# Attention into a gated MLP on one core: the hidden product of batches 1 to 7 with 512 tokens in one PSUM bank and the last 64 tokens of a batch together

## The chip, the cores and the metric

The kernel runs on one core of one Trainium2 chip. The time is device microseconds of one execution. Engines: PE multiplies matrices, and PEld, its weight loads, overlap it; DVE works on vectors, ACT evaluates functions (exponential, logarithm, sine) and copies, POOL and SP mostly issue transfers. PE writes into PSUM, which in this kernel is used as eight banks of 512 float32 values per partition; ACT and DVE read the results from there. Each engine runs its instructions in the order in which the program gives them, and waits for the others by semaphores that the framework sets.

## What is computed

```python
def _attn_ref(q, k, v, p):                     # 8 batches, 8 heads, 576 tokens, 64 per head; p has 32 rows
    p_packed = sm_attn(p, k, v)                # softmax(scale * p k^T) v
    return sm_attn(q, p_packed, p_packed)      # softmax(scale * q p_packed^T) p_packed

def _moe_ref(x, w_in, w_out):                  # x is 4608 x 512, w_in 512 x 2048, w_out 2048 x 512
    h = x @ w_in
    g = h * np.cos(h)
    return g @ w_out
```

The output of the attention, its heads side by side, is `x`: 8 batches of 576 tokens.

## The kernel before

**Batches and steps.** All loops are unrolled, and the program's order is written out by hand. The first attention of a batch gives `p_packed`; the kernel multiplies it with `w_in` at once (`ppw`, L201), so that the hidden product of a batch is h = PPW times a2n, where a2n holds the normalised weights of the second attention (256 rows, as two halves `y` of 128) for 576 tokens. PPW is made in four parts n of 512 of the 2048 hidden columns. h is made in 16 steps `fc` of 128 hidden columns. A step is two accumulating products (y = 0, 1), then a cosine on ACT (a sine with a shift of pi/2), then a multiplication h * cos(h) on DVE into `gT`. The output product (`out_gen`, L343, matmuls on L351) takes 128 tokens at a time, as 16 matmuls of 512 columns.

**Two forms of a step.** `h_mm` (L256) takes all 576 tokens, as two halves of 288 tokens (a bank takes no more than 512), in a pair of banks: four matmuls, one cosine and one multiplication of 576 columns. It serves batches 1 to 7. `h_one` (L283) takes the first 512 tokens in one bank: two matmuls. The last 64 tokens of all 16 steps are then done together by `h_rest` (L298): 32 matmuls of 64 columns into one pair, one cosine of 1024 columns and one multiplication of 1024. These two serve batch 0.

**The joint tile.** 576 is four times 128 and 64 over. The last 64 tokens of an even batch and the next odd one are put side by side into `joint`, which is a fifth group of 128 tokens for the odd batch. `h_mm` has POOL copy them from `gT` into `joint` after steps 7 and 15 (L274); `h_rest` multiplies straight into it (L309).

**Banks.** Two banks (`O`) serve the output product. The other six are grouped by `banks(pairs)` (L54): it closes the pools of the old grouping and opens `pairs` pairs (`psA`, handed out in turn) and single banks (`psH`, `one()`) from the rest. Batch 0's steps run with `banks(0)`, six singles; from L472 on, `banks(3)`, three pairs, holds to the end. `bank()` takes one of the two `O` banks for other uses.

**A batch's period, from batch 2 on.** Ahead of the slot: the scores of the second attention (`s2`, matmuls on L143, into two pairs; in the period of batch 2 they come a little later, and the scores of the first attention, `s1`, stand at the front), the first two parts of PPW, the next batch's scores, the sums (`sums2`), `normalise` into a2n, and between them portions of the previous batch's output product, `fill(n)`, n matmuls each. Then `slot` (L487): sixteen h steps, with the rest of the output product spread between them by a quota; `heavy` gives a step a larger quota, a part of which comes behind the step's extra work (the hooks). `keep` output matmuls are left for the time after the slot. The hook `tiled` at step 7 makes the third and fourth part of PPW (L213) and the next batch's packed values (`pp`, L186), the latter in the unused end of the pair of step 7 (`spare`). `last`, which stands between the matmuls and the multiplication of step 15, transposes these values (`pp_T`, L198). In slot 1 the hooks are others: `pw2` at step 2, `h_rest(0)` at 4, `pack_p` at 6, transposes of k at 8 and 10.

**Order on the engines around a slot's end.** PE: the matmuls of step 15, the two of `pp_T`, the output matmuls left by the quota, those of `fill(5)` (`fill(4)` before `s1(2)`), the scores, a part of PPW. DVE: the multiplication of step 14, the copy of `ppT`, the multiplication of step 15. ACT: the cosine of step 15, a table load, the exponentials of the scores. POOL: the copies into `joint`, then a copy of one element (`behind`, L96) that waits for a transposing transfer, then loads.

Of the kernel before, what the change touches and what calls it, by code (L numbers as in the profile page):

```python
# [15 lines left out]
def kernel(  # L16
# [37 lines left out]
    def banks(pairs):  # L54

        psum["stack"].close()
        if pairs:
            psum["A"] = psum["stack"].enter_context(tc.tile_pool(name="psA", bufs=pairs, space=PSUM))
        if pairs < 3:
            psum["H"] = psum["stack"].enter_context(tc.tile_pool(name="psH", bufs=6 - 2 * pairs, space=PSUM))  # L60
# [28 lines left out]
    def psa(dt=FP32):  # L89
        return psum["A"].tile([128, 2, 512 if dt == FP32 else 1024], dt, name="psA", tag="A")  # L90
# [32 lines left out]
    def bank(dt=FP32):  # L123
        return O.tile([128, 512 if dt == FP32 else 1024], dt, name="ot", tag="ot")
# [54 lines left out]
    def pp(b, eng=V, own=None):  # L179

        ps = own() if own else psa()[:, 0, :]
        for y in range(2):
            for j in range(C):
                c = 2 * (j % 3) + j // 3
                for x in range(4):
                    nc.tensor.matmul(ps[32 * x:32 * x + 32, y * D:(y + 1) * D],  # L186
                                     a1T[b][0:TP, y, j, 32 * x:32 * x + 32],
                                     bf["v", b][:, 2 * x + y, c * D:(c + 1) * D],
                                     start=(j == 0), stop=(j == C - 1))
        t = pp_sb[b % 2].rearrange("p a d -> p (a d)")  # L190
        copy(eng, t[:, 0:2 * D], ps[:, 0:2 * D])
        copy(eng, t[:, 2 * D:3 * D], ps[:, 0:D])
# [5 lines left out]
            nc.tensor.transpose(ps[:, i * 128:(i + 1) * 128], t[:, i * D:i * D + 128], ident)  # L198
        copy(eng, ppT[b % 2].rearrange("p i x n -> p (i x n)"), ps[:, 0:256])

    def ppw(b, n, eng=None, own=False, later=False, cuts=((0, 512),)):  # L201
        if b not in PPW:
            PPW[b] = ppw_pool.tile([128, 2, DF], BF16, name="PPW", tag="PPW")
        two = isinstance(eng, tuple)
        if own:
            ps = [bank(), bank()]
        else:
            t = psa()
            ps = [t[:, 0, :], t[:, 1, :]]
        for x in range(4):  # L210
            for y in range(2):
                r = slice(64 * y, 64 * y + 64)
                nc.tensor.matmul(ps[y][32 * x:32 * x + 32, :], ppT[b % 2][r, 0, x, :],  # L213
                                 w_in_bf[r, x, n * 512:(n + 1) * 512], start=True, stop=True)

        def evacuate(cuts=cuts):
            if own or two:
                for a, z in cuts:
                    for y in range(2):
                        copy(eng[y] if two else eng, PPW[b][:, y, n * 512 + a:n * 512 + z], ps[y][:, a:z])  # L220
            else:
                copy(eng or (V, ACT)[n % 2], PPW[b][:, :, n * 512:(n + 1) * 512], t)
        if later:
            return [lambda c=c: evacuate((c,)) for c in cuts]
        evacuate()
# [25 lines left out]

    gT, joint = {}, {}

    spare = [None]

    def h_mm(b, fc):  # L256
        if fc == 0:
            g_tile(b)
        ps = psa()
        spare[0] = ps[:, 1, HS:512]  # L260
        for y in range(2):
            for e in range(2):
                nc.tensor.matmul(ps[:, e, 0:HS], PPW[b][:, y, fc * 128:(fc + 1) * 128],  # L263
                                 a2n[b][:, y, e * HS:(e + 1) * HS], start=(y == 0), stop=(y == 1))
        cs = cos_pool.tile([128, S], BF16, name="cosT")
        csv = cs.rearrange("p (e x) -> p e x", e=2)
        ACT.activation(out=csv, in_=ps[:, :, 0:HS], func=AF.Sin, bias=PI_HALF)  # L267

        def rest():
            V.tensor_tensor(out=gT[b][:, fc, :].rearrange("p (e x) -> p e x", e=2),  # L270
                            in0=ps[:, :, 0:HS], in1=csv, op=ALU.mult)
            if fc % 8 == 7:
                j0 = (b % 2) * 64
                G.tensor_copy(out=joint[b // 2][:, fc - 7:fc + 1, j0:j0 + 64],  # L274
                              in_=gT[b][:, fc - 7:fc + 1, 512:576])
        return rest

    def g_tile(b):
        gT[b] = g_pool.tile([128, NFC, S], BF16, name="gT", tag="gT")
        if b % 2 == 0:  # L280
            joint[b // 2] = j_pool.tile([128, NFC, 128], BF16, name="joint", tag="joint")

# [15 lines left out]
    def h_rest(b):  # L298

        t = psa()  # L300
        for fc in range(NFC):
            for y in range(2):
                nc.tensor.matmul(t[:, fc // 8, (fc % 8) * 64:(fc % 8) * 64 + 64],  # L303
                                 PPW[b][:, y, fc * 128:(fc + 1) * 128], a2n[b][:, y, 512:576],
                                 start=(y == 0), stop=(y == 1))
        cs = cos_pool.tile([128, 2, 512], BF16, name="cosR", bufs=1)
        ACT.activation(out=cs, in_=t, func=AF.Sin, bias=PI_HALF)
        j0 = (b % 2) * 64
        V.tensor_tensor(out=joint[b // 2][:, :, j0:j0 + 64],  # L309
                        in0=t.rearrange("p a (f x) -> p (a f) x", x=64),  # L310
                        in1=cs.rearrange("p a (f x) -> p (a f) x", x=64), op=ALU.mult)
# [53 lines left out]
    def to_do():  # L365
        return sum(n for _, n in filler)
# [73 lines left out]
    normalise(0)  # L440
    s1(1)
    ACT.preload_act_table_set(SIN_SET)
    cut_ppw, rest_ppw = ppw(0, 0, V, own=True, later=True, cuts=((0, 128), (128, 512)))
    warm(3, psa()[:, 0, :])
    cut_ppw()
    rest_ppw()
# [3 lines left out]
    for fc in range(13):  # L450
        h_one(0, fc)()()
        if fc in (0, 4, 8):
            ppw(0, 1 + fc // 4, (ACT, ACT if fc == 8 else V), own=True)
    c13 = h_one(0, 13)
    pp(1, ACT, own=bank)
    c13()()
# [30 lines left out]
    def slot(s, hooks, keep=0, heavy={}, last=None):  # L487


        left = to_do() - keep  # L490
        weight = [1 + heavy.get(fc, (0, 0))[0] for fc in range(NFC)]
        for fc in range(NFC):
            rest = h_mm(s, fc)
            if fc == NFC - 1 and last:
                last()
            rest()
            quota = (left * sum(weight[:fc + 1])) // sum(weight) - (left + keep - to_do())
            behind = min(quota, heavy[fc][1]) if fc in heavy else quota
            fill(quota - behind)
            while hooks and hooks[0][0] == fc:  # L500
                hooks.pop(0)[1]()
            fill(behind)

    def pw2(b, n, eng=None):
        ppw(b, n, eng)
        ppw(b, n + 1, eng)

    def tiled(b):


        own, later = spare[0], []
        for n in (2, 3):
            later += ppw(b, n, (ACT, V)[n - 2], later=True)
        later[0]()
        pp(b + 1, V, own=lambda: own)
        later[1]()

    def tk2():
# [8 lines left out]
    def cross(n, b):  # L527
        return lambda: xbar(n, b)

    osb_eng[0] = ACT  # L530
    slot(1, [(2, lambda: pw2(1, 2, (ACT, V))), (4, lambda: h_rest(0)), (6, lambda: pack_p(2, 4)), (7, cross("k", 3)),
             (8, tk2), (9, cross("q", 2)), (10, lambda: pe_T("k", 2, (V, V, ACT), (2,)))], 4, {2: (1, 2), 4: (3, 5)})
    ACT.preload_act_table_set(EXP_SET)
    osb_eng[0] = V
    behind(xT["q", 2][0:1, 0, 0:1])
    load("v", 3)
# [35 lines left out]
        load(n, b)  # L572
    fill(9)
    osb_eng[0] = ACT
    slot(2, [(7, lambda: tiled(2))], 10, {7: (5, 4)}, lambda: pp_T(3, V))

    for s in range(3, B):
        nxt = s + 1 < B
        ACT.preload_act_table_set(EXP_SET)
        osb_eng[0] = V  # L580
        set_filler(s - 1)
        fill(5)
        s2(s)
        ppw(s, 0, V)
        fill(8 if nxt else 9)
        if nxt:
            s1(s + 1)
            ppw(s, 1, V)
            a1_xbar(s + 1)
            xbar("q", s + 1)  # L590
            recips(s + 1)
            if s + 2 < B:
                xbar("k", s + 2)
                behind(xT["k", s + 2][0:1, 0, 0:1])
        else:
            for n in range(1, 4):
                ppw(s, n, V)
        fill(4 if nxt else 5)
        sums2(s, 0)
        fill(5)  # L600
        sums2(s, 1)
        normalise(s)
        ACT.preload_act_table_set(SIN_SET)
        fill(13)
        osb_eng[0] = ACT
        for n, b in (("v", s + 2), ("q", s + 2), ("k", s + 3)):
            if b < B:
                load(n, b)
        if nxt:
            slot(s, [(7, lambda: tiled(s))], 5 if s % 2 else 13, {7: (5, 4)}, lambda: pp_T(s + 1, V))  # L610
        else:
            slot(s, [], 5)
    set_filler(B - 1)
    fill(1000)
    tail_chunk(B - 1, 4)
# [30 lines left out]
```

## Time and profile before

| | |
|---|---|
| median of 3 runs | 244.99 us (244.93 to 245.46) |
| the profiled execution | 245.1 us, of which 243.3 us from the first to the last instruction |
| granted TensorE clock | 0.997 |
| output matmuls, L351, on `gT` | 512, 134.0 us busy |
| cosines, L267 | 112, 72.9 us busy, 652 ns each |
| multiplications, L270 | 112, 83.3 us busy, 757 ns each |
| copies into `joint`, L274 | 14, 8.6 us busy, 618 ns each |
| cosine of `h_rest(0)`, L307 | 1, 1023 ns |
| multiplication of `h_rest(0)`, L309 | 1, 1225 ns |

Slot 1 runs from about 40 to 60 us of the span, slot 2 from 74 to 90, slot 3 from 100 to 116, slots 4 to 6 at 126, 152 and 179, slot 7 from 206 to 221; then comes the output product of batch 7. Busy time of a group is the time in which any of its instructions ran; a mean is from the start to the end of one, so that means add up to more than the busy time where instructions overlap, as they do on PE. "Idle before" is time in which the engine had nothing to do ahead of the group's instructions, with what ended it.

### The profile page before, as it was taken

To read this page: it belongs to the slowest core of one execution; us is meant where nothing else is said; L and a number is where in the kernel's file an instruction comes from. 1 tells how busy PE (TensorE), PEld (TensorE's weight loads), DVE (VectorE), ACT (ScalarE), POOL (GpSimd) and SP (SyncE) were. 2 spreads that over 40 slices of the span, in tenths; PEclk is the share of its full clock that TensorE was granted. 3 is DMA by queue.
4 is the path that set the end of the run, shared out by engine and by line. 5 is a ranking of instruction groups with operands and counts; after the bars stand their busy time and mean duration, and the time that the engine had idled before them with its cause. 6 is when DMAs were issued, how large, how long until landed. Compare 5 with 4: busy or idle time off the path is not lost.

```text
span 243.3 us, 5484 instructions
## 1 busy us (share of the span) xinstructions
PE 233.8 (96%) x2251; PEld 128.9 (53%) x2251; DVE 162.0 (67%) x256; ACT 166.1 (68%) x267; POOL 37.4 (15%) x60
## 2 busy tenths in 40 slices
PE   7789899999999999999999999999999999999994
PEld 3454354566446564556455654655455645665453
DVE  3259997787568795778758675868667878784001
ACT  2349999778478696868787687858796666773110
POOL 8432230210400041004100510030101010011000
PEclk9999999999999999999999999999999999999998
DMA  6999999999799999997999899999292111311133
GB/s 94 203 205 206 204 206 229 199 237 187 163 184 183 219 179 180 197 197 163 158 199 219 162 221 204 188 164 176 66 192 52 31 46 43 86 36 53 46 84 86
DMA packets 64377, 37.37 MB, mean 154 GB/s; under 512 B 36865, under 2 KB 59777, under 8 KB 64353
## 3 DMA queue, kind: packets, MB, share of 16 engines
q0 software_dynamic: 23152, 18.75, 51.0%
q1 hardware_dynamic: 40960, 18.16, 35.9%
q8 instruction: 17, 0.28, 0.4%
q10 hardware_dynamic: 240, 0.13, 0.2%
q14 instruction: 8, 0.06, 0.1%
HBM read 37.22 MB, written 9.44 MB: 192 GB/s over the span
## 4 chain that ended last, share of the span: by engine, by line
PE 82%; DVE 6%; ACT 1%; issue 1%; ACTq 0%
PE ot L351 50%; PE psA L263 22%; DVE gT L295 3%; PE psA L213 3%; PE psA L143 2%; PE psA L239 2%; PE ot L337 1%; PE psA L186 1%; DVE gT L270 1%; DVE PPW L87 1%; ACT cosT L267 1%; ACT cosT L294 0%; PE psA L116 0%; DVE qT L87 0%; PE psA L303 0%
## 5 line engine op out<-in xcount | busy, mean ns | idle before, releaser
L351 PE MATMUL ot<-w_out_bf,gT 128*128 128x512 bf16 x512 | 134.0, 379 | 0.0
L270 DVE TENSOR_TENSOR gT<-psA,cosT 128x576 bf16<-128x576 f32 x112 | 83.3, 757 | 21.0 <-ACT cosT L267 19.9
L267 ACT ACTIVATE cosT<-psA 128x576 bf16<-128x576 f32 x112 | 72.9, 652 | 24.9 <-PE psA L263 23.5
L263 PE MATMUL psA<-a2n,PPW 128*128 128x288 bf16 x448 | 73.3, 286 | 0.0
L351 PEld LDWEIGHTS <-gT 128*128 128x128 bf16 x512 | 48.2, 98 | 39.5 <-issue 4.2
L263 PEld LDWEIGHTS <-PPW 128*128 128x128 bf16 x448 | 43.8, 98 | 30.1 <-issue 0.4
L87 DVE CAST PPW<-psA 128x1024 bf16<-128x1024 f32 (+1 forms) x24 | 26.8, 1131 | 6.4 <-PE psA L213 6.2
L85 ACT COPY osb<-ot 128x512 f32<-128x512 f32 (+1 forms) x23 | 13.1, 569 | 16.2 <-PE ot L351 13.9
L87 DVE COPY osb<-ot 128x512 f32<-128x512 f32 (+2 forms) x15 | 9.7, 645 | 20.4 <-PE ot L337 17.2
L274 POOL COPY joint<-gT 128x512 bf16<-128x512 bf16 x14 | 8.6, 618 | 78.2 <-DVE gT L270 78.2
L249 DVE SCALAR_TENSOR_TENSOR a2n<-a2u,r,lns 128x576 bf16<-128x576 bf16 x16 | 12.4, 814 | 9.6 <-ACT lns L247 9.6
L152 ACT ACTIVATE a<-psA 128x576 bf16<-128x576 f32 x16 | 10.2, 646 | 8.2 <-PE psA L143 8.2
L241 ACT ACTIVATE lns<-psA 128x576 f32<-128x576 f32 x16 | 10.3, 650 | 7.2 <-PE psA L239 6.7
L351 PE MATMUL ot<-w_out_bf,joint 128*128 128x512 bf16 x48 | 12.2, 380 | 0.0
L98 POOL COPY gate<-kT 1x1 bf16<-1x1 bf16 x4 | 0.7, 180 | 72.7 <-DMA kT<-kbf 72.7
L231 ACT ACTIVATE a2u<-psA,rs 128x576 bf16<-128x576 f32 x16 | 11.0, 737 | 1.1 <-PE psA L143 1.0
L247 ACT ACTIVATE lns<-lns 128x576 f32<-128x576 f32 x16 | 10.0, 673 | 0.0
L213 PE MATMUL psA<-w_in_bf,ppT 64*32 64x512 bf16 x224 | 9.8, 379 | 0.0
L295 DVE TENSOR_TENSOR gT<-psH,cosT 128x512 bf16<-128x512 f32 x15 | 9.3, 680 | 0.4 <-ACT cosT L294 0.4
L391 PE MATMUL ot<-wz 128*128 128x512 f32 (+2 forms) x13 | 7.5, 661 | 1.9 <-DVE wz L404 1.7
L294 ACT ACTIVATE cosT<-psH 128x512 bf16<-128x512 f32 x15 | 8.4, 628 | 0.7 <-DVE gT L295 0.4
L289 PE MATMUL psH<-a2n,PPW 128*128 128x512 bf16 x30 | 7.8, 381 | 0.8 <-DVE PPW L87 0.8
(88 smaller groups left out, 170.6 us busy)
## 6 DMA issues: line engine op xcount, KB each, us to landing
kbf<-in_k_dram POOLq DMA_DIRECT2D x8, 576.0 KB, 14.0
vbf<-in_v_dram POOLq DMA_DIRECT2D x8, 576.0 KB, 7.8
qbf<-in_q_dram POOLq DMA_DIRECT2D x8, 576.0 KB, 10.9
out_dram<-osb SPq DMA_DIRECT2D x24, 192.0 KB, 2.6
out_dram<-osb SPq DMA_DIRECT2D x22, 128.0 KB, 2.9
w_in_bf<-in_moe_w_in_dram POOLq DMA_DIRECT2D x4, 512.0 KB, 17.3
w_out_bf<-in_moe_w_out_dram POOLq DMA_DIRECT2D x4, 512.0 KB, 20.8
out_dram<-osb SPq DMA_DIRECT2D x25, 64.0 KB, 2.3
```

Of the source, the lines that this page charges most:

```text
L85: ACT.copy(out=out, in_=in_)
L87: eng.tensor_copy(out=out, in_=in_)
L152: ACT.activation(out=a1[b % 2][:, y, :, 0:TP].rearrange("p (e m) x -> p e m x", e=2), in_=ps[y][:, :, 0:HS].rearrange("p e (m x) -> p e m ...
L213: nc.tensor.matmul(ps[y][32 * x:32 * x + 32, :], ppT[b % 2][r, 0, x, :], w_in_bf[r, x, n * 512:(n + 1) * 512], start=True, stop=True)
L231: ACT.activation(out=a2u[b][:, y].rearrange("p (e x) -> p e x", e=2), in_=ps[y][:, :, 0:HS], func=AF.Exp, scale=rs1[b][:, y:y + 1])
L241: ACT.activation(out=lns[b][:, y].rearrange("p (e x) -> p e x", e=2), in_=ps[:, :, 0:HS], func=AF.Ln)
L249: V.scalar_tensor_tensor(out=a2n[b][:, y], in0=a2u[b][:, y], scalar=r1[b][:, y:y + 1], in1=lns[b][:, y], op0=ALU.mult, op1=ALU.mult)
L263: nc.tensor.matmul(ps[:, e, 0:HS], PPW[b][:, y, fc * 128:(fc + 1) * 128], a2n[b][:, y, e * HS:(e + 1) * HS], start=(y == 0), stop=(y == 1))
L267: ACT.activation(out=csv, in_=ps[:, :, 0:HS], func=AF.Sin, bias=PI_HALF)
L270: V.tensor_tensor(out=gT[b][:, fc, :].rearrange("p (e x) -> p e x", e=2), in0=ps[:, :, 0:HS], in1=csv, op=ALU.mult)
L295: return lambda: V.tensor_tensor(out=gT[b][:, fc, 0:512], in0=ps, in1=cs, op=ALU.mult)
L351: nc.tensor.matmul(pss[c], w, w_out_bf[:, fc, :], start=(fc == 0), stop=(fc == NFC - 1))
```

## The change

Batches 1 to 7 take the form that batch 0 had. `h_mm` and `spare` go; a slot begins with `banks(1)`, one pair and four singles, its steps are `h_one(s, fc)`, each in one single, and `h_rest(s)` comes as a hook: behind step 13 in slot 1, behind step 11 in slots 2 to 7. Ahead of the next batch's scores `banks(3)` makes three pairs again. `gT` shrinks to 512 tokens, and POOL's copies into `joint` go. Within a slot, the fourth part of PPW takes two singles instead of a pair (`own=one`), so it leaves them by two copies of 512 columns rather than one of 1024; the third part has the pair, `pp` and `pp_T` take a single each; `pack_p` and one of the transposes of k in slot 1 do so too. In slot 2 the quota at step 7 becomes (6, 3): a larger share of the output matmuls goes there, three of them behind the hook.

```diff
@@ ppw @@
-    def ppw(b, n, eng=None, own=False, later=False, cuts=((0, 512),)):
+    def ppw(b, n, eng=None, own=None, later=False, cuts=((0, 512),)):
...
         if own:
-            ps = [bank(), bank()]
+            ps = [own(), own()]
@@ h @@
-    spare = [None]
-
-    def h_mm(b, fc):
-        if fc == 0:
-            g_tile(b)
-        ps = psa()
-        spare[0] = ps[:, 1, HS:512]
-        for y in range(2):
-            for e in range(2):
-                nc.tensor.matmul(ps[:, e, 0:HS], PPW[b][:, y, fc * 128:(fc + 1) * 128],
-                                 a2n[b][:, y, e * HS:(e + 1) * HS], start=(y == 0), stop=(y == 1))
-        cs = cos_pool.tile([128, S], BF16, name="cosT")
-        csv = cs.rearrange("p (e x) -> p e x", e=2)
-        ACT.activation(out=csv, in_=ps[:, :, 0:HS], func=AF.Sin, bias=PI_HALF)
-
-        def rest():
-            V.tensor_tensor(out=gT[b][:, fc, :].rearrange("p (e x) -> p e x", e=2),
-                            in0=ps[:, :, 0:HS], in1=csv, op=ALU.mult)
-            if fc % 8 == 7:
-                j0 = (b % 2) * 64
-                G.tensor_copy(out=joint[b // 2][:, fc - 7:fc + 1, j0:j0 + 64],
-                              in_=gT[b][:, fc - 7:fc + 1, 512:576])
-        return rest
-
     def g_tile(b):
-        gT[b] = g_pool.tile([128, NFC, S], BF16, name="gT", tag="gT")
+        gT[b] = g_pool.tile([128, NFC, 512], BF16, name="gT", tag="gT")
@@ slot @@
+        banks(1)
         left = to_do() - keep
...
-            rest = h_mm(s, fc)
+            rest = h_one(s, fc)()
@@ pw2, tiled @@
         ppw(b, n, eng)
-        ppw(b, n + 1, eng)
+        ppw(b, n + 1, eng, own=one)
...
-        own, later = spare[0], []
-        for n in (2, 3):
-            later += ppw(b, n, (ACT, V)[n - 2], later=True)
+        later = ppw(b, 2, ACT, later=True) + ppw(b, 3, V, own=one, later=True)
         later[0]()
-        pp(b + 1, V, own=lambda: own)
+        pp(b + 1, V, own=one)
         later[1]()
@@ slot 1 @@
-    slot(1, [(2, lambda: pw2(1, 2, (ACT, V))), (4, lambda: h_rest(0)), (6, lambda: pack_p(2, 4)), (7, cross("k", 3)),
-             (8, tk2), (9, cross("q", 2)), (10, lambda: pe_T("k", 2, (V, V, ACT), (2,)))], 4, {2: (1, 2), 4: (3, 5)})
+    slot(1, [(2, lambda: pw2(1, 2, (ACT, V))), (4, lambda: h_rest(0)), (6, lambda: pack_p(2, 4, one(BF16))), (7, cross("k", 3)),
+             (8, tk2), (9, cross("q", 2)), (10, lambda: pe_T("k", 2, (V, V, ACT), (2,), own=one)), (13, lambda: h_rest(1))], 4, {2: (1, 2), 4: (3, 5)})
     ACT.preload_act_table_set(EXP_SET)
+    banks(3)
@@ slot 2 @@
-    slot(2, [(7, lambda: tiled(2))], 10, {7: (5, 4)}, lambda: pp_T(3, V))
+    slot(2, [(7, lambda: tiled(2)), (11, lambda: h_rest(2))], 10, {7: (6, 3)}, lambda: pp_T(3, V, own=one))
@@ batches 3 to 7 @@
         ACT.preload_act_table_set(EXP_SET)
+        banks(3)
...
-            slot(s, [(7, lambda: tiled(s))], 5 if s % 2 else 13, {7: (5, 4)}, lambda: pp_T(s + 1, V))
+            slot(s, [(7, lambda: tiled(s)), (11, lambda: h_rest(s))], 5 if s % 2 else 13, {7: (5, 4)},
+                 lambda: pp_T(s + 1, V, own=one))
         else:
-            slot(s, [], 5)
+            slot(s, [(11, lambda: h_rest(s))], 5)
```

The calls of `ppw` for batch 0 say `own=bank` in place of `own=True`, which is the same.

More of the change, by code (lines that the diff above doesn't have):

```diff
@@ L442 @@
     ACT.preload_act_table_set(SIN_SET)
-    cut_ppw, rest_ppw = ppw(0, 0, V, own=True, later=True, cuts=((0, 128), (128, 512)))
+    cut_ppw, rest_ppw = ppw(0, 0, V, own=bank, later=True, cuts=((0, 128), (128, 512)))
     warm(3, psa()[:, 0, :])
@@ L452 @@
         if fc in (0, 4, 8):
-            ppw(0, 1 + fc // 4, (ACT, ACT if fc == 8 else V), own=True)
+            ppw(0, 1 + fc // 4, (ACT, ACT if fc == 8 else V), own=bank)
     c13 = h_one(0, 13)
```

## The prediction

> **What bounds it now.** I read the page's totals, then the groups by line with shapes kept apart, then the chain that ended last in order of time, then the timeline around three places. In the groups below the columns are: line, engine, operation, output<-inputs, shapes, count, busy us and mean ns of one, idle before.
>
> ```profile
> span 243.3 us, 5484 instructions
> PE 233.8 (96%) x2251; PEld 128.9 (53%) x2251; DVE 162.0 (67%) x256; ACT 166.1 (68%) x267; POOL 37.4 (15%) x60
> ...
> L263 PE MATMUL psA<-a2n,PPW 128*128 128x288 bf16 x448 | 73.3, 286 | 0.0
> ...
> L295 DVE TENSOR_TENSOR gT<-psH,cosT 128x512 bf16<-128x512 f32 x15 | 9.3, 680 | 0.4 <-ACT cosT L294 0.4
> ```
>
> PE is busy 96% of the span and its two big groups (L351, L263) stand with no idle time before them. Means of PE mislead, since matmuls overlap; the chain gives what each costs in a full stream:
>
> ```profile
> 46.95 0.93 PE psA L303 x32
> ...
> 115.25 0.49 PE psA L263 x4
> 115.74 0.17 PE psA L198 x2
> 115.92 1.51 PE ot L351 x7
> 117.43 0.37 PE psA L143 x16
> ```
>
> (start, us, what.) A 288-column matmul of h takes 0.49/4 = 0.123 us, a 512-column one 1.51/7 = 0.216, and one of 64 columns 0.93/32 = 0.029. In the stretch from slot 2 to slot 7 nearly every piece of the chain is PE. So only two things count: PE's own work, and any wait put on PE.
>
> **PE's work does not change.** The old h step is 4 x 288 columns, 0.49 us; the new one is 2 x 512, 2 x 0.216 = 0.43. Sixteen of them save 16 x (0.49 - 0.432) = 0.93 us a batch. The added `h_rest` is 32 matmuls, which L303 prices at 0.93. The sum is 0.00 for each of the seven batches; the number of matmuls and weight loads is the same.
> The Trainium skill, "TensorE: Matmul & The Clock Gate", section "LDWEIGHTS (loading the stationary operand)", says that a weight load takes its columns divided by 1.2 GHz and so would make 32 matmuls of 64 columns cost their loads; the L303 piece (0.93 us for 32) is against that here, and it stands below as a rival.
>
> **ACT, DVE, POOL.** On DVE, back to back, an old step takes 0.71 us (two in 1.43 in the chain), a new one 9.3/15 = 0.62; 16 x 0.09 = 1.5 us saved, and one multiplication of 1.23 us (L309, seen once) added. On ACT 0.65 against 0.56 (8.4 us for 15), and one cosine of 1.02 (L307) added. Both engines are busy about three quarters of a slot (12.8 and 12.0 us of the 16.2 us of slot 3), so this lies beside PE's matmuls as a total, and uncovered it would cost at most the 1.23 us a batch; what matters is that 1.02 and 1.23 us come in one lump at step 11, four steps before the slot's end. The POOL copies (L274, 14 x 0.62 us) go; POOL waits 78 us for DVE before them, and behind them stands only the next gate copy, which waits 72.7 us for a transpose anyway. No DMA is added or moved: nothing.
>
> **The stall that goes.** In slot 2 the values for batch 3 (L186) wait for the multiplication of step 7, whose pair they share:
>
> ```profile
> 80.67 1.42 DVE L270 TENSOR_TENSOR gT<-psA,cosT 128x576 bf16<-128x576 f32 x2 [0.27 <-ACT cosT L267]
> ...
> 81.34 0.63 PE L213 MATMUL psA<-w_in_bf,ppT 64*32 64x512 bf16 x16
> ...
> 82.15 0.55 PE L186 MATMUL psA<-vbf,a1T 96*32 96x64 bf16 x48 [0.18 <-DVE gT L270]
> ```
>
> L213 takes 0.55 where nothing waits (107.37 to 107.92 in slot 3), so 0.26 us is lost. After, they use the single bank of step 6: -0.26. The other slots have no such wait.
>
> **The stall that comes.** At each slot's end the banks are regrouped from one pair and four singles to three pairs, and the scores (L143) are the first work in the new grouping. Does that first matmul wait for its own two banks only, or for everything in the old grouping? Before has one comparable regrouping, six singles to three pairs at 35 us:
>
> ```profile
> 33.80 0.86 ACT L85 COPY qT<-psH 128x768 bf16<-128x768 bf16 x1
> 34.11 1.02 DVE L87 COPY qT<-psH 128x768 bf16<-128x768 bf16 x2
> 34.25 0.81 PE L391 MATMUL psH<-wz 128*128 128x512 bf16 x3
> ...
> 35.24 0.17 PEld L143 LDWEIGHTS <-ppT 64*32 64x32 bf16 x16 [0.68 <-ACT qT L85]
> 35.27 0.44 PE L143 MATMUL psA<-qT,ppT 64*32 64x288 bf16 x16 [0.21 <-DVE qT L87]
> ```
>
> Counting 22 singles handed out in turn, the last DVE copy (ends 35.13) reads the third bank, and the first score matmuls write the first two and read only the columns that ACT's copy wrote by 34.66. PE's own work was streamed by 34.25 + 3 x 0.216 = 34.9. Yet all 16 start at 35.24, 0.11 us behind that last copy. That data alone is not the reason is seen in slot 3: step 8 starts at 109.29 on the third part of PPW while DVE writes the fourth until 110.11. So I take it that a regrouping waits for all of the old banks. Inside one grouping it waits bank by bank:
>
> ```profile
> 143.15 0.76 DVE L270 TENSOR_TENSOR gT<-psA,cosT 128x576 bf16<-128x576 f32 x1
> 143.87 0.14 PEld L143 LDWEIGHTS <-ppT 64*32 64x32 bf16 x16 [0.42 <-issue]
> ```
>
> There the scores began before step 15's multiplication had ended (143.91). After, they would wait for it, and it is later, because of the lump. From the end of step 11's matmuls in slot 3 (us): h_rest done 0.93; cosine 0.97 to 1.99; its multiplication 2.03 to 3.25; DVE then runs without a gap (0.62 each, the last 0.07 overlapping): steps 12, 13, 14 begin at 3.18, 3.80, 4.41, the ppT copy at 5.03, step 15 at 5.27 and ends at 5.95. PE meanwhile: 0.93 + 4 x 0.432 + 7 output matmuls x 0.216 = 4.17 at the end of step 15. Before, the scores start 117.36 - 115.74 = 1.62 us behind that point, so they are due at 5.79 and get leave at 5.95 + 0.14 (35.13 to 35.27) = 6.09: **0.30 us lost**. Slots 3 to 6 each have seven output matmuls in that stretch: 4 x 0.30 = 1.20. In slot 2 the new weights (6, 3) leave only five: step 15 ends at 3.74; the ppT transposes need the single of step 12, free at 3.18 + 0.68 + 0.14 = 4.00, and lose 0.35; the scores are due at 5.71: 0.38 more, 0.73 in all. In slot 1 h_rest stands at step 13: step 15 ends at 0.93 + 0.86 + 0.86 = 2.65, its multiplication at 4.48, the scores are due 1.44 behind (60.47 to 61.91): 4.62 - 4.09 = 0.52. Behind the waiting matmul stand PPW's first part and all output matmuls; nothing of it is made up, since PE has no slack later. The regrouping at a slot's beginning costs nothing: the last readers of the pairs are the logarithms, which a2n, and so step 0, needs anyway. **Bounds**: if I am wrong on bank by bank, 0; if DVE is 0.2 us later or earlier at each of the six ends, 2.45 - 1.2 = 1.25 to 2.45 + 1.2 = 3.65.
>
> Two small edits are bounded by nothing and 0.1: PPW's fourth part as two 512-column copies on DVE (2 x 0.60 against 1.22), and step 9, which now waits for the first of them: due 1.5 us behind L186's end, released at 0.15 + 0.33 + 0.60 + 0.14 = 1.2. I take 0.
>
> **Sum.** 1.20 + 0.73 + 0.52 - 0.26 = +2.19 on a span of 243.3, so 245.5; the profiled execution took 245.1 with 1.8 around its span, 0.1 above the median of 244.99. Median after: 244.99 + 2.19 = **247.2**. Its own range: 244.99 + 1.25 - 0.26 = 246.0 to 244.99 + 3.65 = 248.6.
>
> **Rivals.**
> (a) *Waits bank by bank even across the regrouping.* Then the scores' first pair is h_rest's, long free, the second holds steps 13 and 14, and only PPW's first part (0.25 us behind the scores) meets step 15: 4 x 0.05 + 0.13, plus 0.35 in slot 2, less 0.26: +0.4, so **245.4**. For it: the row at 143.87. Against: 35.24. It decides if the releaser of L143 is not step 15.
> (b) *Faster.* Four singles let step n run until the multiplication of step n-4, not n-3, has ended, and DVE has 0.3 us less a slot. Its place is the starts around L213, L186 and L143, its price the waits hidden there: from 35.27 to 239.77 all matmuls at stream rates (560 x 0.216, 448 x 0.123, the rest by their pieces) make about 202.5 us against 204.5, so 2.0 at most; half of it gives **244.0**. It decides if (a)'s releases hold and those 0.42 us gaps before weight loads are waits. Against: the gaps carry "issue", and slots 3 to 6 have no wait for DVE in them.
> (c) *The weight loads of h_rest bind*: 32 x 98 ns (PEld, L303) = 3.1 instead of 0.93, seven times 2.2: **260**. Against it is L303's own piece. That is the rule of the page named above.
>
> **Chances.** Forecast 0.60, (a) 0.24, (b) 0.14, (c) 0.01, a larger stall 0.01. A measurement here tells 0.2% (0.49 us) from nothing. Slower: 0.60 + 0.04 of (a) + 0.02 = 0.66; same: 0.18 of (a); faster: 0.14 + 0.02 of (a) = 0.16. The range takes in (a): 244.6 to 248.6.
>
> **What would show it.** PE's busy time as before (233.8) while the span grows by about 2 us; L143's weight loads released by DVE gT L295, 0.3 to 0.7 us each at five or six ends, and the chain leaving PE there through the multiplications from L309 on; no wait at L186 in slot 2; L303 at 0.93 each of seven new times. If L143 waits for nothing, the step on the regrouping is wrong; if step 15 ends sooner than 1.6 us behind its matmuls, the lump is.

## The result, and the profile after

The changed kernel takes 248.03 us (median of 4 runs, 247.95 to 248.09) against 245.01 (4 runs): a ratio of 1.0119, 95% interval 1.0102 to 1.0137. It is slower by 3.0 us where 2.2 were forecast.

The page's totals of the changed kernel:

```profile
span 246.2 us, 5480 instructions
PE 233.4 (95%) x2251; PEld 112.9 (46%) x2251; DVE 161.8 (66%) x268; ACT 166.4 (68%) x274; POOL 28.9 (12%) x46
```

PE is as busy as before (233.4 against 233.8) while the span grew by 2.9 us: the loss is idle time of PE. Two places hold it. The first was not in the forecast; it is the beginning of slot 1, in the timeline (start, us, engine, line, operation, output<-input, shapes, count, idle before and its releaser):

```profile
39.17 1.55 DVE L249 SCALAR_TENSOR_TENSOR a2n<-a2u,r,lns 128x576 bf16<-128x576 bf16 x2 [1.81 <-ACT lns L247]
...
40.63 1.28 DVE L87 CAST PPW<-psA 128x512 bf16<-128x512 f32 x2
42.03 0.13 PEld L265 LDWEIGHTS <-PPW 128*128 128x128 bf16 x2 [2.05 <-issue]
42.06 0.59 PE L265 MATMUL psH<-a2n,PPW 128*128 128x512 bf16 x2 [1.58 <-DVE PPW L87]
```

The same place in the profile of before:

```profile
39.09 1.55 DVE L249 SCALAR_TENSOR_TENSOR a2n<-a2u,r,lns 128x576 bf16<-128x576 bf16 x2 [1.81 <-ACT lns L247]
...
40.23 0.86 PE L263 MATMUL psA<-a2n,PPW 128*128 128x288 bf16 x4
...
40.55 1.28 DVE L87 CAST PPW<-psA 128x512 bf16<-128x512 f32 x2
```

L263 is the matmul of the old step, L265 that of the new one, in a single (`psH`). Step 0 can start when the first half of a2n is there; before, it did, at 40.23. Now it starts at 42.06, just behind two copies of PPW's second part, which it doesn't read; nor, if the pools lie in the order in which they are opened, does it overwrite the banks that they read.

The second is the end of a slot. This is the chain of waits around the end of slot 5 (start, us, what):

```profile
167.18 0.95 PE psA L279 x32
...
168.15 1.03 ACT cosR L283
...
169.21 1.23 DVE joint L285
170.43 1.65 DVE gT L271 x3
...
172.42 0.61 DVE gT L271
...
173.07 0.44 PE psA L143 x16
```

L279 is `h_rest`, L283 and L285 its cosine and its multiplication, L271 a step's multiplication, L143 the scores. Before, all pieces there were PE's. Now the chain leaves PE with `h_rest`, goes through ACT and DVE, and comes back at the scores, 0.04 us behind the last multiplication.

Each start of a first score matmul (from the timelines), and the distance to the one before it:

| | before | after | distance grew by |
|---|---|---|---|
| s2(1) | 35.27 | 35.36 | |
| s1(2), behind slot 1 | 61.91 | 63.81 | 1.81 |
| s2(3), behind slot 2 | 91.43 | 93.58 | 0.25 |
| s2(4), behind slot 3 | 117.36 | 119.65 | 0.14 |
| s2(5), behind slot 4 | 143.87 | 146.36 | 0.20 |
| s2(6), behind slot 5 | 170.38 | 173.07 | 0.20 |
| s2(7), behind slot 6 | 196.89 | 199.78 | 0.20 |

The sum is 2.80 us, and 0.09 lie ahead of s2(1).

Slot 2 needs a closer look, since its 0.25 is a sum of gains and losses. Its end before, and after:

```profile
89.09 0.65 PE L263 MATMUL psA<-a2n,PPW 128*128 128x288 bf16 x4
89.72 0.27 PE L198 MATMUL psA<-ident,pp_sb 128*128 128x128 bf16 x2
```

```profile
90.83 0.59 PE L265 MATMUL psH<-a2n,PPW 128*128 128x512 bf16 x2
91.59 0.27 PE L198 MATMUL psH<-ident,pp_sb 128*128 128x128 bf16 x2 [0.16 <-DVE gT L271]
91.70 1.67 PE L327 MATMUL ot<-w_out_bf,joint 128*128 128x512 bf16 x7
93.58 0.44 PE L143 MATMUL psA<-qT,ppT 64*32 64x288 bf16 x16 [0.21 <-DVE gT L271]
```

PE's means overlap, so the waits are read from start to start. After, the transposes of `ppT` (L198) start 0.76 us behind step 15, where 0.43 is usual (117.33 to 117.76 in slot 3): 0.33 lost. Before, it was 0.63 where 0.49 is usual (141.66 to 142.15 in slot 4): 0.14 were lost there already. The scores start 1.88 us behind the first of the seven output matmuls, where 1.60 is usual (89.83 to 91.43 before): 0.28 lost. L186 no longer waits its 0.26. Together 0.33 - 0.14 + 0.28 - 0.26 = 0.21, of the 0.25 in the table.

### The profile page after: what moved, and what is told of

It is laid out like the page before. It is cut to its first block, busy times and chain, and to the rows that moved or that the text cites. A ratio compares the mean times of both kernels' runs of the same rounds, so it can differ in the third digit from the quotient of the medians.

```text
span 246.2 us, 5480 instructions
## 1 busy us (share of the span) xinstructions
PE 233.4 (95%) x2251; PEld 112.9 (46%) x2251; DVE 161.8 (66%) x268; ACT 166.4 (68%) x274; POOL 28.9 (12%) x46
## 4 chain that ended last, share of the span: by engine, by line
PE 69%; DVE 14%; ACT 4%; DMA 2%; issue 1%; ACTq 0%
PE ot L327 41%; PE psH L265 16%; DVE gT L271 8%; PE psA L279 3%; DVE joint L285 2%; PE psA L213 2%; DMA out_dram<-osb 2%; PE psA L143 2%; ACT cosR L283 2%; PE ot L313 1%; DVE PPW L87 1%; PE psA L239 1%; PE psH L186 1%; DVE a2n L249 1%; ACT a2u L231 1%
## 5 line engine op out<-in xcount | busy, mean ns | idle before, releaser
L271 DVE TENSOR_TENSOR gT<-psH,cosT 128x512 bf16<-128x512 f32 x127 | 84.4, 688 | 18.3 <-ACT cosT L270 17.4
L270 ACT ACTIVATE cosT<-psH 128x512 bf16<-128x512 f32 x127 | 75.1, 603 | 23.0 <-PE psH L265 21.3
L265 PE MATMUL psH<-a2n,PPW 128*128 128x512 bf16 x254 | 74.6, 380 | 2.4 <-DVE PPW L87 2.4
L265 PEld LDWEIGHTS <-PPW 128*128 128x128 bf16 x256 | 24.5, 98 | 32.9 <-issue 2.7
L87 DVE CAST PPW<-psA 128x1024 bf16<-128x1024 f32 (+1 forms) x18 | 20.2, 1134 | 6.9 <-PE psA L213 6.4
L285 DVE TENSOR_TENSOR joint<-psA,cosR 128x1024 bf16<-128x1024 f32 x8 | 9.8, 1225 | 6.1 <-ACT cosR L283 6.1
L283 ACT ACTIVATE cosR<-psA 128x1024 bf16<-128x1024 f32 x8 | 8.2, 1023 | 3.0 <-PE psA L279 3.0
L279 PEld LDWEIGHTS <-PPW 128*128 128x128 bf16 x256 | 8.6, 98 | 1.9
L279 PE MATMUL psA<-a2n,PPW 128*128 128x64 bf16 x256 | 8.8, 193 | 0.0
L367 PE MATMUL ot<-wz 128*128 128x512 f32 (+2 forms) x13 | 6.9, 619 | 1.9 <-DVE wz L380 1.7
L213 PE MATMUL psA<-w_in_bf,ppT 64*32 64x512 bf16 x176 | 8.5, 380 | 0.0
```

What stands on the lines that cost most here:

```text
L87: eng.tensor_copy(out=out, in_=in_)
L265: nc.tensor.matmul(ps, PPW[b][:, y, fc * 128:(fc + 1) * 128], a2n[b][:, y, 0:512], start=(y == 0), stop=(y == 1))
L270: ACT.activation(out=cs, in_=ps, func=AF.Sin, bias=PI_HALF)
L271: return lambda: V.tensor_tensor(out=gT[b][:, fc, 0:512], in0=ps, in1=cs, op=ALU.mult)
L285: V.tensor_tensor(out=joint[b // 2][:, :, j0:j0 + 64], in0=t.rearrange("p a (f x) -> p (a f) x", x=64), in1=cs.rearrange("p a (f x) -> p ( ...
```

## The experiments

Two theories. **The regrouping**: closing the pools of one grouping of banks and opening those of another makes the first matmul in a new pool wait until everything that read the old banks has ended, whichever bank it itself uses. **Bank by bank**: each tile waits for its own banks, and the loss lies in the new steps or in the lump that `h_rest` puts on ACT and DVE, whatever the pools.

### The kernel before, its grouping closed and opened again

At a slot's beginning (`e1_reopen_start`):

```diff
     def slot(s, hooks, keep=0, heavy={}, last=None):
+        banks(3)
         left = to_do() - keep
```

> The kernel before, with its three pairs closed and opened again as the same three pairs at each slot's beginning; no other instruction changes. If opening a grouping waits for every reader of the old one, step 0 of slot 1 must wait for the late copies of PPW's second part on DVE, which end at 41.83 in the trace of before, instead of starting at 40.23: +1.5 us, in slot 1 alone (in the later slots those copies are over long before), so 246.5. If waits go bank by bank, nothing changes: 245.0.

Measured: 246.65 us against 245.18 (ratio 1.0059, interval 1.0042 to 1.0076): +1.47. The timeline of this run:

```profile
40.52 1.28 DVE L87 CAST PPW<-psA 128x512 bf16<-128x512 f32 x2
41.91 0.37 PEld L263 LDWEIGHTS <-PPW 128*128 128x128 bf16 x4 [1.99 <-issue]
41.94 0.65 PE L263 MATMUL psA<-a2n,PPW 128*128 128x288 bf16 x4 [1.53 <-DVE PPW L87]
```

These are the old steps in the old pairs. In slot 1 every tile also has its old pair: six pairs have been handed out since L472, so the turn stands at the first one with or without the reopening. The only thing done is to close and reopen, and step 0 waits for the copies. Bank by bank falls with this.

At the slots' ends (`e2_reopen_end`):

```diff
     ACT.preload_act_table_set(EXP_SET)
+    banks(3)
     osb_eng[0] = V
...
         ACT.preload_act_table_set(EXP_SET)
+        banks(3)
         osb_eng[0] = V
```

> The kernel before, with its three pairs closed and opened again as the same three pairs behind each of slots 1 to 6. If opening a grouping waits for every reader of the old one, the scores wait for step 15's multiplication, which in before ends 0.05 us ahead to 0.04 us behind their start, plus 0.14 us of signal: 0.18, 0.08, 0.00, 0.18, 0.07 and 0.18 us at the six ends, +0.7 in all, so 245.7. Bank by bank: 245.0. It shows what a regrouping costs where nothing lumpy stands ahead of it.

Measured: 245.32 against 245.18 (1.0013, 0.9999 to 1.0027): 0.1, not 0.7. The wait is there, but shorter than I took it. The timeline at the end of slot 4:

```profile
143.03 0.76 DVE L270 TENSOR_TENSOR gT<-psA,cosT 128x576 bf16<-128x576 f32 x1
143.84 0.14 PEld L143 LDWEIGHTS <-ppT 64*32 64x32 bf16 x16 [0.51 <-DVE gT L270]
```

The multiplication ends at 143.79 and the scores start at 143.84, 0.05 us later; I had counted 0.14. The distances of the table grow by 0.08, 0.09 and 0.10 at the ends of slots 1, 4 and 6 and by 0.01 or nothing at the others; at the end of slot 3 the scores wait for nothing (their usual 0.42 us gap). So a regrouping by itself costs a slot's end at most 0.1 us in the old kernel.

### The changed kernel with the late copies moved up

`e3_ppw_early`:

```diff
     fill(3)
+    rest_ppw()
     normalise(1)
     ACT.preload_act_table_set(SIN_SET)
-    rest_ppw()
```

> The changed kernel, with the copies of PPW's second part of batch 1 ahead of the normalisation instead of behind it. If step 0 of slot 1 waits for these copies because of the regrouping (42.06 in the trace of after, 40.23 in before), it now waits only for a2n, which comes some 0.3 us later since DVE does the copies first: 1.4 us come back, 246.6. If the start of slot 1 is late for another reason (single banks as such, the weights), it stays at 248.0.

Measured: 246.61 us (1.0061, 1.0046 to 1.0076 of before), 1.42 under the changed kernel. The start of slot 1 was 1.4 us of the 3.0; the table says the same, 1.81 less the 0.39 that the next run finds at that slot's end.

### The changed kernel with the lump two steps earlier

`e4_rest_early`:

```diff
-    ... (13, lambda: h_rest(1)) ...
+    ... (11, lambda: h_rest(1)) ...
...
-    ... (11, lambda: h_rest(2)) ...
+    ... (9, lambda: h_rest(2)) ...
...
-    ... (11, lambda: h_rest(s)) ...
+    ... (9, lambda: h_rest(s)) ...
```

The last of these stands twice, in the call for slots 3 to 6 and in that for slot 7.

> The changed kernel, with the last 64 tokens of a batch two steps earlier in each slot (step 9 instead of 11, in slot 1 step 11 instead of 13). If the waits at the slots' ends come from the lump of 1.02 us on ACT and 1.23 us on DVE that stands four steps ahead of the end, DVE has caught up by then, and the scores wait at most 0.05 to 0.1 us: about 1.2 us come back, 246.8. If the regrouping costs the same whatever stands ahead of it, it stays at 248.0.

Measured: 246.55 us (1.0057, 1.0042 to 1.0072), 1.48 under the changed kernel. The end of slot 3 in its timeline:

```profile
114.69 3.07 DVE L271 TENSOR_TENSOR gT<-psH,cosT 128x512 bf16<-128x512 f32 x5
...
117.68 0.28 DVE L87 COPY ppT<-psH 128x256 bf16<-128x256 bf16 x1
...
117.88 0.68 DVE L271 TENSOR_TENSOR gT<-psH,cosT 128x512 bf16<-128x512 f32 x1
118.76 0.14 PEld L143 LDWEIGHTS <-ppT 64*32 64x32 bf16 x16 [0.42 <-DVE gT L271]
```

Step 15's multiplication ends at 118.56, 0.2 us ahead of the scores; in the changed kernel it ended 0.06 us ahead of them and held them. The distances between the scores fall by 0.39, 0.31 and four times 0.16 or 0.17 against the changed kernel. The regrouping alone is not enough for a wait at a slot's end: it takes a DVE that is late, and in slots 1 and 3 to 6 the lump made it so.

Slot 2 is different. What came back there is the wait of the transposes (L198), not that of the scores:

```profile
90.98 1.67 PE L327 MATMUL ot<-w_out_bf,joint 128*128 128x512 bf16 x7
92.86 0.44 PE L143 MATMUL psA<-qT,ppT 64*32 64x288 bf16 x16 [0.21 <-DVE gT L271]
```

The scores start 1.88 us behind the start of the output matmuls, as in the changed kernel: 0.28 us too late. Two steps are not enough for DVE to catch up there.

### Both, and a pair that stays open

`e5_both_early` is the two edits together.

> The changed kernel with both: the copies of PPW's second part of batch 1 ahead of the normalisation, and the last 64 tokens two steps earlier in each slot. If the loss is made of two separate waits at regroupings, what each edit alone brought back adds: 1.42 + 1.48 = 2.90 of the 3.0 us, so 245.1, level with the kernel before. If both edits ease the same wait, less: 246.0 or more.

Measured: 245.36 against 245.15 (1.0003, 0.9987 to 1.0019). The edits add up; what remains is level with the kernel before.

`e6_pair_open` leaves both late things where they are and takes one pair out of the regrouping:

```diff
     def banks(pairs):
...
-        if pairs:
+        psum["k"], psum["pairs"] = 0, pairs
+        if psum.get("first") == "due":
+            psum["first"] = ctx.enter_context(tc.tile_pool(name="psF", bufs=1, space=PSUM))
+        if psum.get("first"):
+            if pairs == 3:
+                psum["A"] = psum["stack"].enter_context(tc.tile_pool(name="psA", bufs=2, space=PSUM))
+        elif pairs:
...
     def psa(dt=FP32):
+        k = psum["k"]
+        psum["k"] += 1
+        if psum.get("first") and (k % 3 == 0 or psum["pairs"] == 1):
+            return psum["first"].tile([128, 2, 512 if dt == FP32 else 1024], dt, name="psF", tag="F")
         return psum["A"].tile([128, 2, 512 if dt == FP32 else 1024], dt, name="psA", tag="A")
...
+    psum["first"] = "due"
     banks(3)
...
+    psum["stack"].close()
```

> The changed kernel, with one pair of banks in a pool of its own that is never closed, and only the other four banks regrouped (two pairs or four singles). The order of the work and the bank of each tile stay. The first four heads of the scores behind a slot go to that pair. If it is the closing and opening that makes the scores wait, they now wait for h_rest's multiplication only, and the other four heads, 0.2 us later, for step 15: the waits of 0.4, 0.5 and 4 x 0.2 us at the six ends fall by about 0.2 each, 1.2 in all: 246.8. The start of slot 1 stays late, since PPW's second part lies in the regrouped banks. If the scores wait because of the lump as such, whatever the pools, it stays at 248.0.

Measured: 247.25 us (1.0074, 1.0047 to 1.01), 0.8 under the changed kernel, of 1.2 expected. The timeline shows what the total can't (`psF` is the pair that stays open; lines stand ten further down):

```profile
118.73 0.68 DVE L281 TENSOR_TENSOR gT<-psH,cosT 128x512 bf16<-128x512 f32 x1
119.30 0.28 PEld L153 LDWEIGHTS <-ppT 64*32 64x32 bf16 x16 [0.42 <-DVE ppT L93]
119.30 0.32 PE L153 MATMUL psF<-qT,ppT 64*32 64x288 bf16 x8
...
119.47 0.32 PE L153 MATMUL psA<-qT,ppT 64*32 64x288 bf16 x8
```

The first eight matmuls of the scores, into the open pair, start while step 15's multiplication still runs (it ends at 119.41). The other eight, into a pair that was opened anew, start 0.06 us behind it. At the end of slot 1 it is plainer: the first eight start at 63.47, the others at 63.87, again 0.05 us behind the end of the multiplication, where 0.13 us lie between them when nothing waits. Same engine, same instruction, same moment: the pool decides. Their banks don't explain it: by the count of singles handed out in slot 1, step 15 has the fourth, and these eight go to the pair made of the first two (if pools lie in the order in which they are opened, which no trace shows). The total gained less than expected because the second eight still wait: only the 0.13 us of the first eight come before them, and slots 3 to 6 had only 0.17 or 0.18 to give.

`e7_all` is all three edits.

> All three edits together. What is left of the waits at the slots' ends after the first two (0.2 us in slot 2, 0.1 or less in the others) should go, and the stall that the change took out of slot 2 (0.26 us) then shows: 244.7 to 244.9, a little under the kernel before. If the single banks cost something by themselves, it stays above 245.0.

Measured: 245.23 against 245.15 (1.0004, 0.9982 to 1.0025): not under the kernel before. From s2(1) to s1(2) it takes 26.87 us where before took 26.64: the early copies make a2n late, and step 0 waits 0.3 us for it. From there to s2(4) it takes 55.23 where before took 55.45. Gone from slot 2 are L186's wait of 0.26 and the 0.14 that the transposes of `ppT` lost before; the second eight of the scores still wait 0.15 there (91.46, where 91.31 would do).

`e8_ppw_in_pair` therefore puts the copies back behind the normalisation, and PPW's second part into the pair that stays open:

```diff
+    psum["k"] = 6
     rest_ppw, = ppw(1, 1, (V, V), later=True)
     fill(3)
-    rest_ppw()
     normalise(1)
     ACT.preload_act_table_set(SIN_SET)
+    rest_ppw()
```

The lines are marked against `e7_all`; the count 6 makes the next pair handed out the open one.

> One pair never closed and the last 64 tokens two steps earlier, as before; but the copies of PPW's second part of batch 1 are back behind the normalisation, as late as in the changed kernel, and that part now lies in the pair that is not regrouped. If slot 1 was late only because the copies' bank was closed, its step 0 starts with a2n again, 1.5 us earlier than in the changed kernel although the copies are as late, and the 0.3 us that the early copies cost a2n come back as well: 244.9 to 245.0, 0.2 to 0.3 under the kernel with all three edits. If step 0 waits for the copies whatever their bank, about 246.7.

Measured: 244.93 against 245.07 (0.9998, 0.9988 to 1.0008). Its timeline at the beginning of slot 1:

```profile
38.85 1.55 DVE L259 SCALAR_TENSOR_TENSOR a2n<-a2u,r,lns 128x576 bf16<-128x576 bf16 x2 [1.81 <-ACT lns L257]
...
40.20 0.62 PE L275 MATMUL psH<-a2n,PPW 128*128 128x512 bf16 x2
40.31 1.28 DVE L93 CAST PPW<-psF 128x512 bf16<-128x512 f32 x2
```

Step 0 starts at 40.20, ahead of the copies, which are as late as ever. With that the loss of 3.0 us is gone, and nothing is won: the median is 0.14 us under that of the kernel before, within the interval. The profiled execution took 245.46, more than the median: in slot 2 it waits 0.58 us at L196 (L186 of before) for a transposing transfer into `a1T`, which no other trace here does. No version here beats the kernel before by what can be measured.

## Why the prediction was right, and where it was not

**PE's work: right.** Sixteen new steps at 0.43 and `h_rest` at 0.93 were to equal sixteen old ones at 0.49. The chain has L279 at 0.93 to 0.95 at seven of its eight places (in slot 3 it runs elsewhere; there L279 takes 0.93 from its start to the next matmul's, 113.59 to 114.52), PE's busy time moved by 0.4 us in 234, and with the waits gone (`e8_ppw_in_pair`) the time is that of before.

**A regrouping waits for all of the old banks: right**, by one row of before at 35 us; `e1_reopen_start` shows it with nothing else changed, and `e6_pair_open` within one set of score matmuls. Rival (a), bank by bank, would have given 245.4; it falls.

**The regrouping at a slot's beginning costs nothing: wrong**, and this is the step that failed. I wrote that the last readers of the pairs are the logarithms, which step 0 needs anyway. In slots 2 to 7 nothing is lost indeed, since the program puts the copies of PPW ahead of the normalisation, on the same engine: in slot 2 the last of them ends at 74.51, and step 0 starts with a2n at 76.20. In slot 1 the last reader is the pair of copies of PPW's second part, which the program puts behind the normalisation; before, only step 2 took that pair. It cost 1.42 us by `e3_ppw_early`, and 1.47 in the old kernel by `e1_reopen_start`: half of the loss. The rule that I had applied to the slots' ends was not applied, slot by slot, to their beginnings.

**The slots' ends: right in mechanism, too large.** Forecast were 0.52 (slot 1), 0.73 (slot 2) and 4 x 0.30: 2.45 us. Measured against the usual 1.60 us from the first of the seven output matmuls to the scores, slot 1 lost 0.40 and slots 3 to 6 lost 0.17 or 0.18 each. The mis-sized term is the signal: I took 0.14 us from the end of a multiplication to the scores, from the row at 35 us; at the slots' ends it is 0.05 or 0.06 (119.59 to 119.65, 63.76 to 63.81). The forecast's own row of slot 2 had that too: L186 starts at 82.15, 0.06 behind the multiplication that ends at 82.09. Less 0.09, slot 1 comes to 0.43 and slots 3 to 6 to 0.21.
In slot 2 the working has a slip: 4.00 less 3.74 is 0.26, not 0.35, as the wait of the transposes; the sum of 0.73 holds even so, since it is the time of leave, 6.09, less 3.74 + 1.62. Measured were 0.33 for the transposes and 0.28 for the scores. Overlooked was that the transposes lost 0.14 in before already (89.09 to 89.72), so that only 0.47 are new.

**The stall that goes: right, but not alone.** The packed values of batch 3 (L186 in slot 2) wait for nothing after the change: 0.26, as forecast. With the lump early the 0.14 of the transposes go as well; `e7_all` gains 0.22 us over slots 2 and 3, with 0.15 of wait left.

**ACT, DVE, POOL: right.** The copies into `joint` on POOL went and nothing moved; POOL's gate copies wait 85.0 us for the transposes of k instead of 72.7.

**Rivals (b) and (c).** The extra depth of four singles gained nothing that shows: with the waits gone, `e7_all` and `e8_ppw_in_pair` are level with before. The weight loads don't bind `h_rest`: 256 of them at 98 ns each lie in eight stretches of 0.93 to 0.95. So the rule of the Trainium skill ("TensorE: Matmul & The Clock Gate", "LDWEIGHTS (loading the stationary operand)") does not set the time here.

The total was within its range by luck: 1.4 us were left out at the beginning of slot 1, and the ends were put about 0.8 us too high (2.19 forecast with the stall that goes, 2.80 - 1.42 = 1.38 measured).

## What to carry to other kernels

Here, closing and opening a pool was a barrier for the first tile in the new pool, against the slowest reader of the old one. Look at both ends of every region so grouped for work that was put late on purpose, and keep a tile whose reader is late, or the tile that is needed first, in a pool that stays open.
An equal sum of PE time says nothing about a change that turns sixteen small evacuations into smaller ones and a lump: place the lump so that the engines that carry it have caught up before anything waits for them.

## What had not been expected of the hardware

From the end of DVE's last read to PE's first matmul it took 0.05 to 0.06 us at the slots' ends (143.79 to 143.84, 63.76 to 63.81, 119.59 to 119.65), but 0.14 to 0.15 at the beginning of slot 1 and at 35 us (41.91 to 42.06, 41.80 to 41.94, 35.13 to 35.27). The latter three wait for a copy, but a copy as such is not slow to release, nor is an idle PE slow to start: in the changed kernel a step of batch 0 starts at 27.84, 0.06 us behind the end of DVE's copy at 27.78, after PE had been idle for 0.64 us. What makes the difference was not tried.
Weight loads of 128 columns in a row of 64-column matmuls are 98 ns long each and still follow each other at 0.029 us: 98/29, so they overlap one another more than three deep.
